# Spreading one row of Q over the partitions: by a store and a 128-fold load in place of a matmul

## The chip, the cores and the metric

The kernel runs on one core of a Trainium2 chip. The core has five instruction streams that the profile names: TensorE (PE, with its weight loads as PEld), VectorE (DVE), ScalarE (ACT), GpSimd (POOL) and SyncE (SP), which here only issues transfers; a "q" behind the name (SPq) is the engine's sequencer. The metric is the device time of one execution in microseconds (us). Lower is better.

## The reference: what is computed

```python
def _attn_ref(x):                       # x: (8, 3008, 256)
    X = np.fft.fft(x, axis=1)
    X = np.fft.fft(X, axis=2)
    return X.real.astype(np.float32)

def _moe_ref(x, w_gate, w_val, w_out):  # x: (24064, 256), d_ff = 1536
    g = x @ w_gate
    silu = g * (1.0 / (1.0 + np.exp(-g)))
    val = x @ w_val
    return (silu * val @ w_out).astype(np.float32)
```

The real part of a two-dimensional Fourier transform over sequence and model dimension goes, as 8 x 3008 = 24064 rows of 256, through a gated feed-forward block. Inputs and output are f32 in device memory.

## The kernel before, in words

The transform over the sequence is done by matmuls with tables of sines and cosines, after the input rows have been folded by their symmetry. The transform over the model dimension is multiplied into the weights once, at the start. Symmetry also halves the rest: for each pair of mirrored output rows the kernel holds one column of `Pt` (cosine part) and one of `Qt` (sine part), both bf16 with 128 partitions; the row is one combination of the two and its mirror row the other. There are 8 x 1504 = 12032 such columns.

They are cut into 24 tiles: tile 0 and tile 3 of 480 columns, tile 23 of 320 (and 8 special columns behind them), the others of 512. For each tile the loop goes over the 12 blocks of 128 hidden features. One (tile, block) is a *unit*, `(t, f)`; there are 288, written out in program order by the loop at lines 930 to 960. Each engine runs its own instructions in that order and waits on semaphores for the others.

A unit has these parts:

- `part_a` (lines 746 to 791): matmuls of the gate `g` and the value `v` (line 756), Silu on ACT, the product `hp` for the row.
- `part_b` (lines 793 to 808), one unit later: the matmuls that turn the accumulated sums into the mirror row's (line 799), Silu again, the product `hm`.
- `OWork` (lines 695 to 726): of the tile before, eight 128x256 output matmuls (line 722) per unit. A pair of 128-row blocks is ready every three units; `evict` (line 679) copies it from PSUM to a buffer `ev` on ACT (line 682; the pool has four buffers, line 649) and SP stores it (line 688).
- At some units, the fold of later input on POOL (lines 160 to 191), loads of `XA` and `XC` for it on SP's queue (lines 128 to 147, dealt out by `run_loads`, line 835), and `transform` (line 566), which makes the next tiles' `Pt` and `Qt`; DVE writes them at line 611. A tile's last `Qt` columns are written at units 5 and 6 of the tile before, at the latest.

From tile 3 on, some units are *split* (lines 733 to 744 and 762 to 784): blocks 0, 2, 4, 6, 8 and 10, and in the last tiles eight of twelve. There the value's even part `e` and odd part `o` are kept apart: DVE forms `es = bc * w0[f] + e` (line 769), then `vp = es - o/2` (line 775) and `vm = es + o/2` (line 778 or 781), and POOL multiplies by the Silu.

`bc` is row 0 of `Qt` (the model dimension's term d = 0) on all 128 partitions. `spread_row0` (line 920) makes it: a matmul with `sel`, whose row 0 is all ones and the rest zero, into a PSUM tile of the pool `o` (line 923), and an ACT copy to SBUF in f32 (line 926). It is called for tile 3 ahead of unit (3, 0), and for each tile t + 1 from 4 to 23 ahead of unit (t, 11), the last of the tile before: 21 times. The first reader is line 769 of the next tile's unit 0. The pool `bc` has two buffers.

SP's queue is in order: it issues the output stores, each after ACT's copy, and the input loads, each after its buffer is free. Transfers on this queue take turns on eight semaphores, and each waits for the eighth before it.

Of the kernel before, what the change touches and what calls it, by code (L numbers as in the profile page):

```python
# [12 lines left out]
F32 = mybir.dt.float32  # L13
I32 = mybir.dt.int32
BF16 = mybir.dt.bfloat16
# [16 lines left out]
def kernel(  # L32
# [8 lines left out]
    nc = tc.nc  # L41
    B, M, D = x.shape
    Dff = moe_w_gate.shape[1]
    P = 128
# [4 lines left out]
    nF = Dff // P  # L49
    T = 512  # L50
# [6 lines left out]
    nT = len(wide)  # L57
# [9 lines left out]
    def width(t):  # L67
        return wide[t]
# [22 lines left out]
    sel = const.tile([P, P], BF16, name="sel")  # L91
# [24 lines left out]
    def rows_at(b, row, ap):  # L116
        return bass.AP(tensor=x.tensor, offset=(b * M + row) * D, ap=ap)
# [4 lines left out]
    def down_set(b, a, j, L, n):  # L122

        return rows_at(b, R * (a + 1) - 2 * j, [[2 * L * D, n], [-2 * D, L], [1, 2 * D]])
# [125 lines left out]
    for hi in range(2):  # L250
        q.dma_start(out=XC3[64 * hi:64 * hi + NCR, 0:2, :],
                    in_=rows_at(0, 2 * (P + 1) - 1 + 2 * hi * R, [[2 * D, NCR], [R * D, 2], [1, 2 * D]]))
    for hi in range(2):
        for a in range(2):
            q.dma_start(out=XC3[64 * hi:64 * hi + NCR, 2 + a, :],
                        in_=down_set(0, 3 - 2 * hi - a, JC, LC, NC_))
    q.dma_start(out=XC0[NCR:64 + NCR + 1:64, 0:2, 1],
                in_=rows_at(0, 0, [[2 * R * D, 2], [R * D, 2], [1, D]]))
# [21 lines left out]
    for i in range(6):  # L280
        ps = psO.tile([P, T], F32, name="o")
# [253 lines left out]
    def pq_tiles(t):  # L535
        if t not in ptile:
            w = width(t) + B if t == nT - 1 else T
            ptile[t] = (pqp if t < nT - 1 else const).tile([P, w], BF16, name="Pt")
            qtile[t] = (pqp if t < nT - 1 else const).tile([P, w], BF16, name="Qt")
        return ptile[t], qtile[t]  # L540
# [101 lines left out]

    hp = ctx.enter_context(tc.tile_pool(name="ht", bufs=2))
    sgp = ctx.enter_context(tc.tile_pool(name="sg", bufs=3))
    sgv = ctx.enter_context(tc.tile_pool(name="sgv", bufs=4))
    esp = ctx.enter_context(tc.tile_pool(name="es", bufs=2))
    bcp = ctx.enter_context(tc.tile_pool(name="bc", bufs=2))
# [42 lines left out]
    def run_evicts():  # L690
        for fn in evicts:
            fn()
        evicts.clear()
# [36 lines left out]
    state = {}  # L730
    owork = None

    SPLIT = {0: "H", 2: "H", 4: "P", 6: "P", 8: "P", 10: "H"}
    SPLIT_END = {0: "P", 1: "P", 3: "P", 4: "P", 6: "P", 7: "P", 9: "P", 10: "P"}
    t_end = tile_of((B - 1) * H) - 1

    bc = {}

    def split(u):

        t, f = u
        if t < 3 or (t == nT - 1 and f > 9):
            return None
        return (SPLIT if t < t_end else SPLIT_END).get(f)

# [47 lines left out]
    def part_b(u):  # L793
        t, f = u
        w = width(t)
        Pt, Qt = pq_tiles(t)
        g, v = state.pop(u)
        for gv, ps in ((0, g), (1, v))[:1 if split(u) else 2]:
            nc.tensor.matmul(ps[:, :w], Wm[:, gv, f * P:(f + 1) * P], Qt[:, :w], start=False, stop=True,  # L799
                             skip_group_check=True)  # L800
        if split(u) == "P":
            sg = sgv.tile([P, T], F32, name="sgv")
            nc.scalar.activation(sg[:, w - 1::-1], g[:, :w], AF.Silu)  # L803
            nc.gpsimd.tensor_tensor(hts[t][1][:, f, :w], sg[:, :w], v[:, :w], op=Alu.mult)  # L804
            return
        sg = sgp.tile([P, T], F32, name="sg")
        nc.scalar.activation(sg[:, :w], g[:, :w], AF.Silu)  # L807
        nc.vector.tensor_tensor(hts[t][1][:, f, w - 1::-1], sg[:, :w], v[:, :w], op=Alu.mult)  # L808
# [26 lines left out]
    def run_loads(i):  # L835

        if not loads:
            credit[0] = 0
            return
        credit[0] += 7 if loads[0][0][0] == "A" else 5 if i >= 2 * nF else 12  # L840
        while loads and credit[0] >= loads[0][2]:
            credit[0] -= loads[0][2]
            loads.pop(0)[3]()
# [7 lines left out]
    def items_a(b):  # L851
        return [(("A", b), 0, 2 if k < NA else 4, fn) for k, fn in enumerate(load_a(b, nc.sync))]
# [6 lines left out]
    def fold_step(what, i, unit):  # L859
        kind, b = what  # L860
        q, j = divmod(i, 6)
        if j == 0:
            load_all(what, q)
            if kind == "A":
                queue[what] = fold_steps(nc.gpsimd, XA, *coef_a(b), q, slice(0, P))
            else:
                bb = 1 if b == 1 else q
                queue[what] = fold_steps(nc.gpsimd, XC, *coef_c(b), bb, slice(0, P), q_down=bb)
        queue[what].pop(0)()
        if q == LASTQ[kind, b == 1] and j == 0:  # L870
            act_at.setdefault(max(unit + 2, 11), []).append(what)

    def load_next(what):
        kind, b = what
        if kind == "A":
            if b + 1 < B:
                at = next((k for k, ((kd, c), *_) in enumerate(loads) if kd == "C" and c > b + 1), len(loads))
                loads[at:at] = items_a(b + 1)
        else:
            b = b // 2 * 2 + 2  # L880
            if b < B:
                loads.extend(items_c(b))
# [36 lines left out]

    def spread_row0(t):  # L920
        ps = psO.tile([P, T], F32, name="o")
        w = width(t) + (B if t == nT - 1 else 0)
        nc.tensor.matmul(ps[:, :w], sel, pq_tiles(t)[1][:, :w], start=True, stop=True)  # L923
        bc.pop(t - 2, None)
        bc[t] = bcp.tile([P, T], F32, name="bc")
        nc.scalar.copy(bc[t][:, :w], ps[:, :w])

    prev = None
    owork = None
    for i, u in enumerate(units):  # L930
        t, f = u
        if (t, f) == (3, 0):
            spread_row0(t)
        if 3 <= t < nT - 1 and f == nF - 1:
            spread_row0(t + 1)
        for fn in before.pop(i, ()):
            fn()
        if i == 10:
            loads[0:0] = items_a(1)
        run_loads(i)  # L940
        odd = part_a(u)
        if owork:
            owork.run(4)
        if odd:
            odd()
        if prev is not None:
            part_b(prev)
            run_evicts()
            if prev[1] == nF - 1:
                owork = OWork(prev[0], hts[prev[0]])  # L950
                owork.run(4)
        if owork and not (prev is not None and prev[1] == nF - 1):
            owork.run(4)
        for what, j in fold_at.get(i, ()):
            fold_step(what, j, i)
        for what in act_at.pop(i, ()):
            load_next(what)
        if i in job_at:
            transform(*job_at[i])
        prev = u  # L960
# [38 lines left out]
```

## Time and profile before

| | |
|---|---|
| median of 3 runs | 665.38 us (665.36 to 665.39) |
| profiled execution | 665.54 us |
| its span, first to last instruction | 663.8 us |
| granted TensorE clock, mean | 0.999 |
| PE busy | 652.4 us (98%) |
| DVE busy | 541.2 us (82%) |
| POOL busy | 482.5 us (73%) |
| ACT busy | 427.7 us (64%) |
| bytes moved by DMA | 52.56 MB, mean 79 GB/s |

The busy time of an engine is the union of its instructions' times. Matmuls overlap their neighbours, so a single matmul's length in the profile is longer than the distance from its start to the next one's. "A <- B" in a list of waits means that an instruction of A stood idle until B had finished; the figures are the sum in us, the times it happened and the longest. In the chain of work that ended last, each step is followed back to what released it. A timeline row has the start in us, the length in us, engine, line, operation, output and inputs, and a count of merged instructions. Rows by window have the window, its length, then the busy time and count of PE, PEld, DVE, ACT and POOL, the granted clock, the DMA engines' busy share and GB/s.

### The profile page before, as it was taken

To read this page: it belongs to the slowest core of one execution; us is meant where nothing else is said; L and a number is where in the kernel's file an instruction comes from. 1 tells how busy PE (TensorE), PEld (TensorE's weight loads), DVE (VectorE), ACT (ScalarE), POOL (GpSimd) and SP (SyncE) were. 2 spreads that over 40 slices of the span, in tenths; PEclk is the share of its full clock that TensorE was granted. 3 is DMA by queue.
4 is the path that set the end of the run, shared out by engine and by line. 5 is a ranking of instruction groups with operands and counts; after the bars stand their busy time and mean duration, and the time that the engine had idled before them with its cause. 6 is when DMAs were issued, how large, how long until landed. Compare 5 with 4: busy or idle time off the path is not lost.

```text
span 663.8 us, 13324 instructions
## 1 busy us (share of the span) xinstructions
PE 652.4 (98%) x4366; PEld 413.0 (62%) x4366; DVE 541.2 (82%) x976; ACT 427.7 (64%) x762; POOL 482.5 (73%) x507
## 2 busy tenths in 40 slices
PE   7999999999999999999999999999999999999997
PEld 5446666666656666666666666656666666666676
DVE  7786668888888888888888888888889888888872
ACT  7576566666666666666666666666666666666663
POOL 9890952988678789785786777885776668877871
PEclk9999999999999999999999999999999999999999
DMA  9554223525312261245225211124111111111112
GB/s 231 105 93 114 75 88 89 159 71 121 109 56 64 78 150 60 64 108 124 60 67 136 76 33 49 35 77 128 49 33 49 33 46 35 49 32 49 48 49 73
DMA packets 49767, 52.56 MB, mean 79 GB/s; under 512 B 7130, under 2 KB 41026, under 8 KB 49698
## 3 DMA queue, kind: packets, MB, share of 16 engines
q1 hardware_dynamic: 46514, 49.35, 27.3%
q0 software_dynamic: 3184, 2.36, 2.4%
q8 instruction: 34, 0.56, 0.4%
q14 instruction: 35, 0.29, 0.2%
HBM read 29.39 MB, written 24.65 MB: 81 GB/s over the span
## 4 chain that ended last, share of the span: by engine, by line
PE 93%; DMA 3%; DVE 2%; SPq 1%; issue 0%; ACT 0%; DVEq 0%; ACTq 0%
PE o L722 37%; PE g L756 18%; PE v L756 18%; PE g L799 9%; PE v L799 5%; PE v L579 3%; DMA XC<-in_x_dram 2%; PE g L579 1%; DMA XA<-in_x_dram 1%; PE o L923 1%; SPq L144 1%; DVE Qt L611 1%; DVE hp L790 0%; DVE hm L808 0%; SPq L141 0%
## 5 line engine op out<-in xcount | busy, mean ns | idle before, releaser
L782 POOL TENSOR_TENSOR hp<-sgv,vv 128x512 bf16<-128x512 f32 (+2 forms) x135 | 169.1, 1252 | 109.2 <-DVE vv L775 94.9
L807 ACT ACTIVATE sg<-g 128x512 f32<-128x512 f32 (+2 forms) x201 | 118.8, 591 | 83.0 <-PE g L799 66.0
L722 PE MATMUL o<-Wo,hp 128*128 128x256 bf16 (+2 forms) x1140 | 169.6, 273 | 0.0
L722 PE MATMUL o<-Wo,hm 128*128 128x256 bf16 (+2 forms) x1140 | 169.6, 273 | 0.0
L808 DVE TENSOR_TENSOR hm<-sg,v 128x512 bf16<-128x512 f32 (+2 forms) x201 | 135.1, 672 | 21.9 <-ACT sg L807 21.9
L722 PEld LDWEIGHTS <-hp 128*128 128x128 bf16 (+2 forms) x1140 | 112.0, 98 | 63.5
L722 PEld LDWEIGHTS <-hm 128*128 128x128 bf16 (+2 forms) x1140 | 112.0, 98 | 63.2 <-issue 0.4
L769 DVE SCALAR_TENSOR_TENSOR es<-bc,w,v 128x512 f32<-128x512 f32 (+2 forms) x135 | 98.7, 731 | 30.3 <-PE v L756 30.1
L804 POOL TENSOR_TENSOR hm<-sgv,vv 128x512 bf16<-128x512 f32 (+2 forms) x87 | 107.0, 1239 | 16.9 <-ACT sgv L803 16.4
L790 DVE TENSOR_TENSOR hp<-sg,v 128x512 bf16<-128x512 f32 (+2 forms) x153 | 102.6, 671 | 13.4 <-ACT sg L789 11.4
L789 ACT ACTIVATE sg<-g 128x512 f32<-128x512 f32 (+2 forms) x153 | 90.3, 590 | 31.4 <-PE g L756 29.7
L756 PE MATMUL g<-Pt,Wp 128*128 128x512 bf16 (+2 forms) x288 | 108.2, 376 | 0.3 <-DVE Qt L611 0.3
L756 PE MATMUL g<-Qt,Wq 128*128 128x512 bf16 (+2 forms) x288 | 107.9, 375 | 0.5 <-DVE Qt L611 0.5
L756 PE MATMUL v<-Pt,Wp 128*128 128x512 bf16 (+2 forms) x288 | 107.9, 375 | 0.0
L799 PE MATMUL g<-Qt,Wm 128*128 128x512 bf16 (+2 forms) x288 | 107.8, 374 | 0.0
L775 DVE SCALAR_TENSOR_TENSOR vv<-v,es 128x512 f32<-128x512 f32 (+2 forms) x135 | 91.8, 680 | 17.9
L766 ACT ACTIVATE sgv<-g 128x512 f32<-128x512 f32 (+2 forms) x135 | 80.0, 593 | 23.2 <-PE g L756 18.2
L756 PEld LDWEIGHTS <-Wp 128*128 128x128 bf16 x576 | 56.3, 98 | 43.9 <-issue 7.4
L803 ACT ACTIVATE sgv<-g 128x512 f32<-128x512 f32 (+2 forms) x87 | 50.8, 584 | 47.3 <-PE g L799 39.4
L799 PE MATMUL v<-Qt,Wm 128*128 128x512 bf16 (+2 forms) x153 | 57.3, 374 | 2.1 <-DVE hp L790 2.1
L756 PEld LDWEIGHTS <-Wq 128*128 128x128 bf16 x441 | 43.2, 98 | 24.1 <-issue 0.9
L778 DVE SCALAR_TENSOR_TENSOR vv<-v,es 128x512 f32<-128x512 f32 (+2 forms) x87 | 57.6, 662 | 0.0
(173 smaller groups left out, 721.5 us busy)
## 6 DMA issues: line engine op xcount, KB each, us to landing
out_dram<-ev SPq DMA_DIRECT2D x96, 128.0 KB
XA<-in_x_dram SPq DMA_DIRECT2D x32, 256.0 KB
XA<-in_x_dram SPq DMA_DIRECT2D x112, 64.0 KB
XC<-in_x_dram SPq DMA_DIRECT2D x210, 16.0 KB
XC<-in_x_dram SPq DMA_DIRECT2D x56, 60.0 KB
out_dram<-ev SPq DMA_DIRECT2D x12, 120.0 KB
out_dram<-ev SPq DMA_DIRECT2D x10, 112.0 KB
XA<-in_x_dram SPq DMA_DIRECT2D x1, 1024.0 KB
```

Source lines behind the costliest of these rows:

```text
L722: nc.tensor.matmul(ps[:n, j, :], hts[minus][:, f, c:c + n], Wo[:, f, :], start=(f == 0), stop=(f == nF - 1))
L756: nc.tensor.matmul(ps[:, :w], Wt[:, gv, fs], src[:, :w], start=start, stop=stop, skip_group_check=True)
L766: nc.scalar.activation(sg[:, :w], g[:, :w], AF.Silu)
L769: stt(es[:, :w], bc[t][:, :w], w0[:, f:f + 1], e[:, :w], op0=Alu.mult, op1=Alu.add)
L775: stt(vp[:, :w], o[:, :w], -0.5, es[:, :w], op0=Alu.mult, op1=Alu.add)
L782: nc.gpsimd.tensor_tensor(hts[t][0][:, f, :w], sg[:, :w], vp[:, :w], op=Alu.mult)
L789: nc.scalar.activation(sg[:, :w], g[:, :w], AF.Silu)
L790: nc.vector.tensor_tensor(hts[t][0][:, f, :w], sg[:, :w], v[:, :w], op=Alu.mult)
L799: nc.tensor.matmul(ps[:, :w], Wm[:, gv, f * P:(f + 1) * P], Qt[:, :w], start=False, stop=True, skip_group_check=True)
L804: nc.gpsimd.tensor_tensor(hts[t][1][:, f, :w], sg[:, :w], v[:, :w], op=Alu.mult)
L807: nc.scalar.activation(sg[:, :w], g[:, :w], AF.Silu)
L808: nc.vector.tensor_tensor(hts[t][1][:, f, w - 1::-1], sg[:, :w], v[:, :w], op=Alu.mult)
```

## The change

From tile 4 on the matmul and the ACT copy go. In their place `store_row0(t + 1)` ahead of unit (t, 7) stores partition 0 of `Qt` (up to 512 bf16, 1 KB) to a buffer in device memory, and `load_row0(t + 1)` ahead of unit (t, 9) loads that row into all 128 partitions of a `bc` tile (128 KB written). Both are issued on SP's queue; the load waits for the store's landing, and behind it in the queue stand the loads of that unit and the output stores of unit 9. `bc` becomes bf16, as `Qt` is. Line 769 of the next tile waits for the load. Tile 3 keeps its matmul, with a bf16 copy. A new pool `rd` of two buffers in device memory is added.

```diff
+    rdp = ctx.enter_context(tc.tile_pool(name="rd", bufs=2, space=bass.MemoryType.DRAM))
...
+    ROW0 = (7, 9)
...
     def spread_row0(t):
         ps = psO.tile([P, T], F32, name="o")
+        w = width(t)
+        nc.tensor.matmul(ps[:, :w], sel, pq_tiles(t)[1][:, :w], start=True, stop=True)
+        bc[t] = bcp.tile([P, T], BF16, name="bc")
+        nc.scalar.copy(bc[t][:, :w], ps[:, :w])
+
+    row0d = {}
+
+    def store_row0(t):
         w = width(t) + (B if t == nT - 1 else 0)
-        nc.tensor.matmul(ps[:, :w], sel, pq_tiles(t)[1][:, :w], start=True, stop=True)
-        bc.pop(t - 2, None)
-        bc[t] = bcp.tile([P, T], F32, name="bc")
-        nc.scalar.copy(bc[t][:, :w], ps[:, :w])
+        row0d[t] = rdp.tile([1, T], BF16, name="row0")
+        nc.sync.dma_start(out=row0d[t][:, :w], in_=pq_tiles(t)[1][0:1, :w])
+
+    def load_row0(t):
+        w = width(t) + (B if t == nT - 1 else 0)
+        bc[t] = bcp.tile([P, T], BF16, name="bc")
+        nc.sync.dma_start(out=bc[t][:, :w], in_=row0d.pop(t)[0, :w].partition_broadcast(P))
...
-        if 3 <= t < nT - 1 and f == nF - 1:
-            spread_row0(t + 1)
+        if 3 <= t < nT - 1 and f in ROW0:
+            (store_row0, load_row0)[ROW0.index(f)](t + 1)
```

## The prediction

> **What bounds the kernel now.** I read the page first (busy shares, granted clock, the chain that ended last), then the waits of TensorE (PE), then PE's own instructions around the removed one.
>
> ```profile
> span 663.8 us, 13324 instructions
> PE 652.4 (98%) x4366; PEld 413.0 (62%) x4366; DVE 541.2 (82%) x976; ACT 427.7 (64%) x762; POOL 482.5 (73%) x507
> ...
> PEclk9999999999999999999999999999999999999999
> ...
> PE 93%; DMA 3%; DVE 2%; SPq 1%; issue 0%; ACT 0%; DVEq 0%; ACTq 0%
> PE o L722 37%; PE g L756 18%; PE v L756 18%; PE g L799 9%; PE v L799 5%; PE v L579 3%; DMA XC<-in_x_dram 2%; PE g L579 1%; DMA XA<-in_x_dram 1%; PE o L923 1%; SPq L144 1%; DVE Qt L611 1%; DVE hp L790 0%; DVE hm L808 0%; SPq L141 0%
> ```
>
> PE is busy 98% of the span at a full granted clock, and 93% of the chain is PE. Line 923, the matmul that the change removes, is itself on that chain. Busy time can flatter a pipelined engine, so the waits decide. These are PE's waits on other engines from 131 to 652 us, which is tile 4 to just before the drain, and in the same stretch DVE's wait at line 769:
>
> ```profile
> PE v L756 <- DVE vv L778: 1.0, 2, 0.6
> ```
> ```profile
> DVE es L769 <- PE v L756: 29.1, 42, 0.8
> ```
>
> In 521 us PE waited 1.0 us for others, in two places, while DVE, the nearest rival for the bound, waited for PE. So in the tiles that change, the time is the spacing of PE's instructions, and a PE instruction less gains its spacing.
>
> **The change, part by part.**
>
> *Twenty matmuls go (tiles 4 to 23; tile 3 keeps its own).* All 21 of today, their weight loads, and the ACT copies behind them:
>
> ```profile
> L923 PEld LDWEIGHTS <-sel x21: 97/98/98, 103.6 to 629.7; 128*128 128x128 bf16 x21
> L923 PE MATMUL o<-Qt,sel x21: 303/379/379, 103.8 to 629.8; 128*128 128x512 bf16 x19, 128*128 128x480 bf16 x1, 128*128 128x328 bf16 x1
> ```
> ```profile
> L926 ACT COPY bc<-o x21: 432/587/592, 104.2 to 630.2; 128x512 f32<-128x512 f32 x19, 128x480 f32<-128x480 f32 x1, 128x328 f32<-128x328 f32 x1
> ```
>
> The 379 ns is not the price: it is one matmul's length from start to end, and the next starts before it ends. The price is the distance of the starts, from the timeline of PE at the end of tile 5 and of tile 22:
>
> ```profile
> 179.83 0.60 PE L722 MATMUL o<-Wo,hm 128*128 128x256 bf16 x4
> 180.26 0.38 PE L923 MATMUL o<-Qt,sel 128*128 128x512 bf16 x1
> 180.48 0.38 PE L756 MATMUL g<-Pt,Wp 128*128 128x512 bf16 x1
> 180.70 0.38 PE L756 MATMUL g<-Qt,Wq 128*128 128x512 bf16 x1
> 180.91 0.38 PE L756 MATMUL v<-Pt,Wp 128*128 128x512 bf16 x1
> ...
> 629.83 0.30 PE L923 MATMUL o<-Qt,sel 128*128 128x328 bf16 x1
> 629.97 0.38 PE L756 MATMUL g<-Pt,Wp 128*128 128x512 bf16 x1
> ```
>
> From 180.26 to 180.91 are three steps, 0.217 us each. Tiles 4 to 22 are 512 wide: 19 x 0.217 = 4.12 us. Tile 23 has 328 columns: 629.97 - 629.83 = 0.14. Sum 4.26 us, all on the path. The weight loads (98 ns) lie under the matmul before and add nothing; if each stood open, the gain would be 20 x 0.098 = 2.0 us more.
>
> The Trainium skill gives another price: "TensorE: Matmul & The Clock Gate", section "Back-to-back issue gap", has about 131 ns per matmul of 512 columns sustained in a stream with weight loads, and 216 ns for the isolated one. By the first the sum would be an estimated 20 x 0.131 = 2.6 us. The trace has a stream with weight loads at 217 ns, so the trace decides.
>
> *Twenty ACT copies go:* 20 x 0.587 = 11.7 us of ACT, which is 64% busy and not on the chain; worth 0. As cover for PE it only gains. POOL waited for these copies 2.9 us:
>
> ```profile
> POOL hp L782 <- DVE vv L775: 94.9, 71, 3.2
> ...
> POOL hp L782 <- ACT bc L926: 2.9, 3, 1.1
> ```
>
> but POOL waits 94.9 us for DVE in the same list (131 to 663 us), so this too frees nothing. The list holds no wait for a transfer.
>
> *DVE reads bf16 in place of f32* (line 769), and its first such instruction of a tile waits for the load's semaphore:
>
> ```profile
> L769 DVE SCALAR_TENSOR_TENSOR es<-bc,w,v x135: 548/741/749, 104.9 to 647.2; 128x512 f32<-128x512 f32 x122, 128x328 f32<-128x328 f32 x7, 128x480 f32<-128x480 f32 x6
> L769 DVEq EVENT_SEMAPHORE  x1: 50/50/50, 104.8 to 104.8; - x1
> ```
>
> The instruction's other input stays f32 in PSUM; I take its 741 ns unchanged. The extra wait instruction is at most 20 x 0.05 = 1.0 us of DVE, on an engine that has 29.1 us of waits for PE here: 0, with 1.0 us as the upper end.
>
> *Forty transfers join SP's queue.* SP's other work, and where it stands idle:
>
> ```profile
> L688 SPq DMA_DIRECT2D out_dram<-ev x279: 254/359/1224, 59.1 to 660.9; - x140
> ```
> ```profile
> SPq L688 <- ACT ev L682: 299.2, 81, 7.5
> ...
> SPq L141 <- DMA XC<-in_x_dram: 5.8, 11, 0.9
> ```
>
> Issuing costs 40 x 0.36 = 14 us of SP. SP waits 299.2 us for the copies of line 682, up to 7.5 at once, and hides it. The load also waits in SP's queue until its store has landed. Behind it stand the output stores of unit 9 and, in tiles with input traffic, loads of XA and XC. The output stores may be late without harm: evO has four buffers, one taken every three units, so only a delay of many microseconds reaches ACT and then PE. For late input loads the folds on POOL would wait; POOL waits for no transfer in its list above. Cost 0. The store itself waits for DVE's last write of Q, which is done before SP arrives, as the next rows show.
>
> *Does the row arrive in time?* No row shows this pair of transfers, so I bound each landing. SP reaches the store after the output stores of unit 6, and the row is needed at the next tile's first es. Tile 19 to 20 (little traffic), 3 to 4 and 12 to 13 (the heaviest):
>
> ```profile
> 545.25 1.14 SPq L688 DMA_DIRECT2D out_dram<-ev  x3
> ```
> ```profile
> 123.03 1.01 SPq L688 DMA_DIRECT2D out_dram<-ev  x2
> ...
> 359.26 1.61 SPq L688 DMA_DIRECT2D out_dram<-ev  x3
> ```
> ```profile
> 543.04 1.33 DVE L611 TENSOR_TENSOR Qt<-g,od 128x160 bf16<-128x160 f32 x7 [1.21 <-PE g L756]
> ...
> 556.45 0.75 DVE L769 SCALAR_TENSOR_TENSOR es<-bc,w,v 128x512 f32<-128x512 f32 x1 [0.80 <-PE v L756]
> ```
> ```profile
> 131.37 0.74 DVE L769 SCALAR_TENSOR_TENSOR es<-bc,w,v 128x512 f32<-128x512 f32 x1
> ...
> 370.02 0.74 DVE L769 SCALAR_TENSOR_TENSOR es<-bc,w,v 128x512 f32<-128x512 f32 x1
> ```
>
> Q is written by 544.4, SP is free at 546.4, es starts at 556.45: 10.1 us, less two issues of 0.36, leaves 9.3 us for two landings. In tile 12 to 13 it is 370.02 - 360.87 = 9.1 us, in tile 3 to 4 131.37 - 124.04 = 7.3 us. What a landing takes, from the chain (a small load alone; the megabyte and a small load behind it, at the start of the run), and the traffic in the three places:
>
> ```profile
> 1.98 5.97 DMA XA<-in_x_dram
> ...
> 26.50 1.95 DMA XC<-in_x_dram
> ```
> ```profile
> 0.00:25.00 25.00, 21.50 (x145) 13.18 (x146) 16.83 (x59) 16.65 (x24) 22.25 (x49) 1.00 0.91 205
> ...
> 119.00:127.00 8.00, 8.00 (x57) 5.33 (x55) 6.99 (x13) 5.37 (x11) 8.00 (x9) 1.00 0.77 217
> 361.00:368.00 7.00, 7.00 (x46) 4.37 (x45) 5.93 (x10) 4.69 (x9) 6.08 (x8) 1.00 0.75 199
> 545.00:556.50 11.50, 10.89 (x72) 6.86 (x71) 9.72 (x17) 7.37 (x14) 8.20 (x7) 1.00 0.15 46
> ```
>
> (The last two columns are the DMA engines' busy share and GB/s; the first line is the start of the run.) Lower end 1.95 us each, upper end 5.97 us each. In a quiet tile the share is 0.15, so 1.95 is the near row: 2 x 1.95 + 0.7 = 4.6 us of 10.1, some 5 us to spare. In tile 3 to 4 four XA loads (1.05 MB) and two output stores (0.26 MB) go ahead of the row: 1.31 MB at 217 GB/s is 6.0 us from 119.35, plus 1.95, so the store lands near 127.3; the load, 0.4 + 1.95 + 0.6 (128 KB at that rate), near 130.3, about 1 us before es. Tile 12 to 13 has 2 us or more to spare. So 0 in every tile; with the upper end for one of the two landings in the two heavy tiles, 1 to 2 us late in all.
>
> *Sum:* -4.26 us. The profiled execution took 665.54 us (span 663.8 and 1.7 around it), 0.16 above the median of the runs; 665.54 - 4.26 = 661.28, and against the median 661.1.
>
> **Rivals.**
>
> 1. *The row is late in the heavy tiles.* For it: DMA shares of 0.77 and 0.75, and only 7.3 us in tile 3 to 4. Against it: the sums above. It costs some 1.2 us: 662.3. The Trainium skill speaks for it ("DMA: Bandwidth & Descriptors", section "Queues, rings and completion order"): descriptors of one queue are consumed in ring order on each DMA engine, so a small row would queue behind the XA loads; the trace's bytes ahead of it were priced so above.
>
> 2. *The row is late in every tile: slower.* DVE's queue is in order, so a late es holds DVE, then POOL's hp and the v buffers PE needs. It decides where the two landings take over 9.3 us together in quiet tiles, and eats the gain at 9.5 (20 x 0.21 us). At 10 us each tile loses 0.7: 665.4 - 4.3 + 14 = 675. For it: at the upper end, 2 x 5.97 = 11.9, it happens. Against it: that price is from a share of 0.91 at the start of the run, here 0.15.
>
> 3. *No gain:* the tile's pace is DVE's or POOL's, and PE only gets idle time: 665.4. For it: DVE is 82% busy and caused both of PE's waits. Against it: 1.0 us of waits in 521.
>
> 4. *A weight load comes into the open.* Before, the weights of the next tile's first matmul load under line 923 (0.217 us); after, under the last matmul of line 722, whose starts are 0.43 / 4 = 0.109 us apart. If its 98 ns then stand open, a tile gains 0.217 - 0.098 = 0.119 and the whole 2.4 us: 663.0. Against it: 0.098 fits under 0.109, and lines 722 follow each other at that distance all through. The skill's 131 ns, named above, would come to nearly the same time.
>
> 5. *The whole 379 ns is won:* 20 x 0.379 = 7.6 us, 657.8. For it: nothing but the duration row.
>
> **How the numbers follow.** Forecast 0.75; rival 1, 0.08; rival 2, 0.08; rival 3, 0.05; rival 4, 0.03; rival 5, 0.01. Faster by over 0.2% (1.3 us, about what a measurement of this kernel can tell from no change) are the forecast and rivals 1, 4 and 5: 0.87. Same: 0.05. Slower: 0.08. The forecast's own range is 661.1 with 1.0 us down (PE's two waits vanish) and 1.0 us up (the upper end of the wait instructions); I take 660.1 to 663.0, which adds rivals 1 and 4 and leaves out 2, 3 and 5, 0.14.
>
> **What would show it.** Right: line 923 left once, PE's spacing from the last line 722 of a tile to the first line 756 without a gap, PE's waits near 1.0 us, no wait of es on the bc load, SP's wait for line 682 shrunk by roughly the load's wait for its store (20 x 2 us). Wrong: a row "DVE es <- DMA bc", or PE waiting for vv or hp at the first units of a tile, or POOL's L168 waiting for XA or XC.

## The result, and the profile after

The changed kernel takes 661.88 us (median of 4 runs, 661.67 to 662.33) against 665.38 us before: ratio 0.9949, 95% interval 0.9936 to 0.9961, so 3.5 us faster by the medians (2.6 to 4.3 by the interval). In the later series on one chip it is 662.06 against 665.97, ratio 0.9942 (0.9930 to 0.9955), 3.9 us. The forecast was 661.1, a gain of 4.26 us. The direction and the mechanism held; 0.8 us of the gain is missing in the first series and 0.35 us in the second, and the experiments are mostly about that part.

Lines behind the new pool have moved by one to thirteen: 722 is now 723, 756 is 758, 769 is 771, 799 is 801, 803 is 805; the store is line 934 and the load line 939. The page of the changed kernel, answering to the lines shown of before:

```profile
span 659.8 us, 13360 instructions
PE 649.1 (98%) x4346; PEld 411.5 (62%) x4346; DVE 539.4 (82%) x976; ACT 418.1 (63%) x742; POOL 481.7 (73%) x507
...
PE 93%; DMA 3%; DVE 2%; SPq 1%; issue 0%; ACT 0%; DVEq 0%; ACTq 0%
PE o L723 37%; PE g L758 18%; PE v L758 18%; PE g L801 9%; PE v L801 5%; PE v L579 3%; DMA XC<-in_x_dram 2%; PE g L579 1%; DMA XA<-in_x_dram 1%; SPq L144 1%; DVE Qt L611 1%; DVE hp L792 0%; SPq L141 0%; DVE hm L810 0%; PE o L452 0%
```

PE has 20 matmuls fewer, is as busy as before, and the removed line has left the chain; no other line has taken its share. PE's waits on other engines from 131 to 648 us, and DVE's in that stretch:

```profile
PE v L758 <- DVE vv L780: 1.0, 2, 0.6
```
```profile
DVE es L771 <- PE v L758: 28.1, 42, 0.8
...
DVE vv L777 <- POOL BBc L189: 0.5, 1, 0.5
```

PE still waits 1.0 us, in the same two places, and there is no row of es waiting for the load. SP's waits now (the page of its queue):

```profile
SPq L689 <- ACT ev L683: 263.3, 77, 7.5
SPq L939 <- DMA row<-Qt: 10.8, 9, 2.0
```

The wait for ACT's copies is 36 us shorter than before (299.2). Issuing the forty transfers takes 12.3 us of that, and the loads' waits for their stores 10.8 us; the rest lies in other rows of the list. SP had the time.

The seam between tile 5 and tile 6 in PE's timeline:

```profile
179.28 0.60 PE L723 MATMUL o<-Wo,hm 128*128 128x256 bf16 x4
179.72 0.38 PE L758 MATMUL g<-Pt,Wp 128*128 128x512 bf16 x1
179.93 0.38 PE L758 MATMUL g<-Qt,Wq 128*128 128x512 bf16 x1
```

Line 758 starts 0.44 us after the four matmuls of line 723, where line 923 started before. The hole is closed without a gap. I matched PE's 4346 common matmuls one by one in the two traces and noted each place where the distance to the trace of before changes by more than 0.03 us. Behind the noise of the first 16 us there are these:

```
step (us)   times   where
-0.216      19      first matmul of tiles 4 to 22 (-0.215 to -0.216)
-0.139       1      first matmul of tile 23
+0.14        2      transform's gate matmul, line 579, at 223 and 383 us of before
+0.06, +0.07 2      v <- Qt,Wm (line 758), in tiles 8 and 10
start: -0.10        line 402, behind the first XC transfer (15.15 before, 15.05 after)
sum: -3.93
```

### The profile page after: what moved, and what is told of

Read it like the earlier page. It is cut to its first block, busy times and chain, and to the rows that moved or that the text cites. A ratio compares the mean times of both kernels' runs of the same rounds, so it can differ in the third digit from the quotient of the medians.

```text
span 659.8 us, 13360 instructions
## 1 busy us (share of the span) xinstructions
PE 649.1 (98%) x4346; PEld 411.5 (62%) x4346; DVE 539.4 (82%) x976; ACT 418.1 (63%) x742; POOL 481.7 (73%) x507
## 4 chain that ended last, share of the span: by engine, by line
PE 93%; DMA 3%; DVE 2%; SPq 1%; issue 0%; ACT 0%; DVEq 0%; ACTq 0%
PE o L723 37%; PE g L758 18%; PE v L758 18%; PE g L801 9%; PE v L801 5%; PE v L579 3%; DMA XC<-in_x_dram 2%; PE g L579 1%; DMA XA<-in_x_dram 1%; SPq L144 1%; DVE Qt L611 1%; DVE hp L792 0%; SPq L141 0%; DVE hm L810 0%; PE o L452 0%
## 5 line engine op out<-in xcount | busy, mean ns | idle before, releaser
L810 DVE TENSOR_TENSOR hm<-sg,v 128x512 bf16<-128x512 f32 (+2 forms) x201 | 135.1, 672 | 20.9 <-ACT sg L809 20.9
L771 DVE SCALAR_TENSOR_TENSOR es<-bc,w,v 128x512 f32<-128x512 bf16 (+2 forms) x135 | 98.8, 732 | 29.3 <-PE v L758 29.1
L758 PE MATMUL v<-Qt,Wq 128*128 128x512 bf16 (+2 forms) x153 | 57.4, 375 | 0.0
```

The source lines that it names most:

```text
L758: nc.tensor.matmul(ps[:, :w], Wt[:, gv, fs], src[:, :w], start=start, stop=stop, skip_group_check=True)
L771: stt(es[:, :w], bc[t][:, :w], w0[:, f:f + 1], e[:, :w], op0=Alu.mult, op1=Alu.add)
```

## The experiments

**The changed kernel again, and four ways to take it apart.** The later series named above, five rounds on one chip, has this run and the next ones, up to the kernel with both matmuls and transfers, all against the same runs of the kernel before (665.97 us). The first of it is the changed kernel itself.

> The changed kernel once more, to see how far its single times lie apart (661.67 to 662.33 so far, against 665.36 to 665.48 before the change). Theory A, the gain is the 20 removed matmul spacings less two waits of the transform's gate matmul for a PSUM buffer that the planner chose otherwise (0.14 us each): 661.4 in most executions, and a later one needs another cause. Theory B, the transfers cost time by their traffic and their place in SP's queue: 661.7 to 662.3, spread over 0.5 us. Theory C, the row is late for line 771 in some executions: the same spread, with a wait of es for the bc load in a profile that is slow.

Measured: 662.06 us (661.92 to 662.40), 3.9 us under before. The kernel before spread here from 665.28 to 666.21, as widely as any variant, so theories B and C lose the argument they had from the spread. C loses its other sign too: this profile has no wait of es for the load, and the row lands at least 1.01 us before es in every tile. A's absolute figure missed: the whole series, the kernel before included, runs 0.6 us later than the first one. By the gain, A expected 4.0 us and 3.9 were measured. Part of the scatter can be seen: in the profiles of this series line 402, near the beginning, starts anywhere from 15.18 to 15.51 us.

**Neither matmul nor transfers.** From tile 4 on this kernel leaves out each tile's own row 0: line 769 reads the row of tile 3.

```diff
+    bcfix = bcp.tile([P, T], BF16, name="bcfix")
...
-        bc[t] = bcp.tile([P, T], BF16, name="bc")
-        nc.scalar.copy(bc[t][:, :w], ps[:, :w])
+        for k in range(t, nT):
+            bc[k] = bcfix
+        nc.scalar.copy(bcfix[:, :w], ps[:, :w])
+        nc.scalar.copy(bcfix[:, w:], zero.to_broadcast([P, T - w]))
...
-        if 3 <= t < nT - 1 and f in ROW0:
-            (store_row0, load_row0)[ROW0.index(f)](t + 1)
```

> Neither matmul nor transfers from tile 4 on: line 769 reads tile 3's row in every tile, so the d=0 term is left wrong. This measures the removed matmuls alone; the planner's PSUM buffers are those of before. All theories: 665.4 - 4.26 = 661.1, single times within 0.15 us. If it is 661.7 or more, the matmuls were worth less than their spacing.

Measured: 661.49 us (661.35 to 661.78), 4.48 under before, ratio 0.9934 (0.9921 to 0.9948). The profiled span is 659.6 against 663.8, 4.2 us. The removed matmuls are worth their spacing, as all theories had it by the gain; the absolute 661.1 is missed with the whole series, and the single times lie 0.43 us apart where I expected 0.15.

**Transfers, but nobody reads the row.** As the last, with the calls of store and load kept and the load going into a tile of its own:

```diff
-        bc[t] = bcp.tile([P, T], BF16, name="bc")
-        nc.sync.dma_start(out=bc[t][:, :w], in_=row0d.pop(t)[0, :w].partition_broadcast(P))
+        bcu[t] = bcp.tile([P, T], BF16, name="bc")
+        nc.sync.dma_start(out=bcu[t][:, :w], in_=row0d.pop(t)[0, :w].partition_broadcast(P))
```

> Stores and loads as in the change, but nothing reads the loaded row (line 769 reads tile 3's), and the planner's PSUM buffers are those of before. Theory A: 661.1, as with neither. Theory B, traffic and SP's queue cost: 661.6 to 662.0, with the spread of the changed kernel. Theory C, late rows: 661.1 and no spread, since nobody waits for the row.

Measured: 661.52 us (661.15 to 661.93), 4.45 under before, ratio 0.9935 (0.9922 to 0.9947). The absolute figure is near theory B's 661.6, but the kernel with neither stands at 661.49 in the same series: beside it, the transfers cost 0.03 us. Matched matmul by matmul, the two traces differ by one step over 0.03 us: 0.10 at line 402, before the first store. Theory B falls.

**Matmuls and transfers.** The kernel before, with the store and the load added beside its matmul and copy:

```diff
+        if 3 <= t < nT - 1 and f in ROW0:
+            (store_row0, load_row0)[ROW0.index(f)](t + 1)
...
+        bcu[t] = bup.tile([P, T], BF16, name="bu")
+        nc.sync.dma_start(out=bcu[t][:, :w], in_=row0d.pop(t)[0, :w].partition_broadcast(P))
```

> The kernel before with its matmuls and copies kept (bc in bf16), and the same stores and loads added beside them into a tile that nothing reads. Theories A and C: 665.4, as before. Theory B: 665.9 to 666.3.

Measured: 665.79 us (665.63 to 666.24), ratio 1.0000 (0.9991 to 1.0008). The same answer from the other side: matched with the trace of before, it ends 0.22 us later, and 0.22 us is the step at line 402. Its profile has PE's wait unchanged at 1.0 us (131 to 652 us):

```profile
PE v L761 <- DVE vv L783: 1.0, 2, 0.6
```

So what the changed kernel (662.06) loses against the unread row (661.52) goes with the reading, as far as it is not scatter. The matched traces of these two differ by 0.61 us: 0.14 at each of the two gate matmuls, 0.07 and 0.05 in tiles 8 and 10, and 0.21 at line 402, near the beginning, which varies from run to run. That leaves 0.40 us for the reading. At the first gate matmul, PE in the trace of before and in the changed kernel's, and ACT in the latter:

```profile
223.06 0.33 PE L579 MATMUL v<-Tab,CEa 128*128 128x189 bf16 x2
223.23 0.33 PE L560 MATMUL v<-Tab,CEa 128*128 128x189 bf16 x2
223.39 0.33 PE L579 MATMUL g<-Tab,CEa 128*128 128x189 bf16 x2
```
```profile
222.08 0.33 PE L579 MATMUL v<-Tab,CEa 128*128 128x189 bf16 x2
222.25 0.33 PE L560 MATMUL v<-Tab,CEa 128*128 128x189 bf16 x2
222.55 0.33 PE L579 MATMUL g<-Tab,CEa 128*128 128x189 bf16 x2
```
```profile
221.90 0.60 ACT L805 ACTIVATE sgv<-g 128x512 f32<-128x512 f32 x1 [0.55 <-PE g L801]
```

Before, the gate matmul follows line 560 after 0.16 us. After, it comes 0.30 us behind and starts at 222.55, just when the Silu of line 805 ends (221.90 + 0.60 = 222.50). The built programs tell why: the pool of gate accumulators has three PSUM buffers, and here two are about to come free, one that DVE frees and one that this Silu frees. Before, the planner gave the transform the first, and it does so in the kernels where nothing reads the loaded row; where line 771 depends on the load it gives it the second, here and once more at 383 us. Of the main loop's buffers none other moved but those of the gate (from the first of these points to the second) and of the output accumulators, which lost the removed tile.

**The buffers put back.** The transforms of unit (7, 5) and (13, 5) take over the gate tile of the transform one unit earlier:

```diff
-        ps = given or {eo: [pool.tile([P, T], F32, name=nm) for pool, nm in ((psV, "v"), (psG, "g"))] for eo in eos}
+        ps = given or {eo: [psV.tile([P, T], F32, name="v"), gkeep.pop((b, part), None) or psG.tile([P, T], F32, name="g")]
+                        for eo in eos}
+        if (b, part) in ((3, 0), (5, 0)) and eos == (0,) and not given:
+            gkeep[b, part] = ps[0][1]
```

> The change, with the PSUM buffers of the gate put back to those of before: the transform at unit (7, 5) and the one at (13, 5) take over the gate buffer of the transform one unit earlier, which DVE frees, in place of the one that ACT's mirror Silu frees. Theory A: the two waits of 0.14 us go, the starts of PE stand as with the unread row, and the time is 0.3 to 0.4 us under the changed kernel's, some 661.5 to 661.7 where the kernel before takes 665.97. If the difference between the changed kernel and the unread row (0.5 us) comes from waiting for the row: no better than the changed kernel, 662.0.

Measured: 661.67 us (661.60 to 661.91) against 665.80, ratio 0.9937 (0.9923 to 0.9951). In PE's timeline the gate matmul is back at its distance (line 579 is 584 here):

```profile
222.59 0.33 PE L584 MATMUL v<-Tab,CEa 128*128 128x189 bf16 x2
222.75 0.33 PE L560 MATMUL v<-Tab,CEa 128*128 128x189 bf16 x2
222.92 0.33 PE L584 MATMUL g<-Tab,CEa 128*128 128x189 bf16 x2
```

Matched against the unread row, both steps of 0.14 us are gone and the small ones in tiles 8 and 10 remain (0.06 and 0.08). The trace settles it. The time agrees in direction (4.13 us under before, where the changed kernel was 3.91 under), but the intervals overlap, so the 0.2 us cannot be told by times alone. Its median is the lowest of the kernels here that compute the whole reference.

**The row brought later.** The same change with other units, one round each.

```diff
-    ROW0 = (7, 9)
+    ROW0 = (9, 11)
```

> The load two units later (store ahead of unit 9, load ahead of unit 11), so it stands behind the output stores of unit 9. In the changed kernel's trace these end some 3.2 us before es in quiet tiles, and a load takes 2.9 us: margin about 0 to 0.3 us, and none where XA and XC loads stand between. If the row's lateness is what decides: 662 to 666, with waits of es for the bc load in busy tiles. If the row has more time than its landing shows: 662.0.

Measured: 682.24 us (681.51 to 682.96), ratio 1.0246 (1.0226 to 1.0265): slower than before, and far outside what I expected. DVE's waits in its profile:

```profile
DVE es L771 <- PE v L758: 28.1, 43, 1.3
DVE es L771 <- DMA bc<-row: 20.3, 12, 3.6
```

By the landing of each load (the last update of its semaphore in the trace) es starts 0.10 us behind it in 19 of the 20 tiles: these now wait for their row. In tile 15 es starts 0.28 us behind the landing and no later than in the changed kernel. My margin of 0 to 0.3 us took the load's landing as 2.9 us everywhere; it was 2.9 to 4.1 here, and between the output stores of unit 9 and the load stand the input loads of unit 10 in busy tiles.

How much of the lateness PE pays can be read tile by tile. I took as lateness how much later than in the changed kernel es starts behind the matmul `v <- Pt,Wp` before it (0.34 to 0.57 us there), and as loss how much longer it takes from that matmul to the next tile's. Es is late by 24.4 us in all, up to 3.6 in a tile, and the loss is 19.5 us: in most tiles the lateness less 0.3 us. (The wait row's 20.3 us counts 12 of the tiles only; that it comes so near to 682.24 - 661.88 = 20.4 us of time is chance.)

```diff
-        if 3 <= t < nT - 1 and f in ROW0:
-            (store_row0, load_row0)[ROW0.index(f)](t + 1)
+        if 3 <= t < nT - 1 and f == 11:
+            store_row0(t + 1)
+            load_row0(t + 1)
```

> Store and load both ahead of unit 11, behind the output stores of unit 9. The landing of the store (1.3 us) now comes on top: the row lands about 1.2 us after es could start in quiet tiles, 2 us in busy ones. If a late es holds PE by its full lateness: 662 + 20 x 1.2 = 686, slower than before. If the v buffers give PE slack for part of it: between 670 and 680. It tells where rival 2 begins and what a late row costs per microsecond.

Measured: 716.95 us (716.15 to 717.74), ratio 1.0767 (1.0746 to 1.0787). DVE's wait for the load and PE's for es:

```profile
DVE es L771 <- DMA bc<-row: 47.8, 17, 5.1
```
```profile
PE v L758 <- DVE es L771: 33.0, 19, 4.1
PE v L758 <- DVE hm L810: 4.1, 11, 0.4
PE v L758 <- DVE vv L780: 3.7, 7, 0.6
```

55 us over the changed kernel, 2.75 us per tile, where I had 1.2 to 2. By the same reckoning es is late by 53.0 us in all (1.0 to 5.2 in a tile) and the loss is 54.1 us. The v buffers give PE little slack, some 0.3 us in a tile: then PE stands at the next line 758 for es itself, and what is later than that passes through one to one. Five tiles lose more than their lateness; the last section comes back to them.

## Why the prediction was right

*What bounds the kernel:* right. PE's starts set the time, and with 1.0 us of waits on other engines in 521 us every PE instruction taken out in tiles 4 to 23 came off the time. Rival 3, no gain, is out.

*The price of the matmuls:* right to 0.02 us. The steps are 19 x 0.216 and 0.139, together 4.24 us, where the prediction had 4.26 from three distances of starts. The kernel with neither confirms it by time (4.48, with an interval of 3.5 to 5.3) and by span (4.2). The length of 379 ns (rival 5) would have given 7.6. The isolated gap of 216 ns in the Trainium skill, "TensorE: Matmul & The Clock Gate", section "Back-to-back issue gap", is what this stream shows, weight loads and all; its sustained 131 ns per matmul is not, and neither is rival 4, since no weight load came into the open.

*ACT's copies, the bf16 read:* worth 0, as said. Line 771 has the mean of 732 ns that line 769 had with 731.

*Forty transfers in SP's queue:* cost 0, as said, shown twice: 0.03 us without the matmuls and -0.18 us (ratio 1.0000) with them, and no step in the matched traces behind line 402. SP's wait for the copies shrank by 36 us, near the 40 us foretold (20 x 2 us), but that is partly luck: the loads stood only 10.8 us for their stores, in nine of the tiles from 14 on, since in the others input loads fill the time between store and load.

*Whether the row arrives in time:* right, and rival 1 did not happen. The landings in the changed kernel's trace, from the updates of the semaphores:

```
tile   store lands after   load issued   load lands   es starts   margin (us)
 4     2.45                126.09        129.18       131.04      1.85
 8     1.37                230.11        234.25       236.82      2.57
13     1.37                361.97        366.00       368.02      2.01
20     1.90                545.25        548.10       553.08      4.99
22     1.28                596.49        599.37       604.55      5.18
```

Tile 4 and tile 13 have the least, as the bounds had it (about 1 us and 2 us or more); quiet tiles have 3.4 to 5.4 where the prediction had some 5. Tile 4 has little to spare: 1.01 us in the second profile of this kernel and 0.49 us in that with the buffers put back. Stores landed in 1.1 to 2.5 us, with the lower bound of 1.95 between; loads took 2.8 to 4.1, well above it, and nowhere the upper bound of 5.97.

*Rival 2* did not happen, but as a mechanism it is real: two units later it makes the kernel slower than before. The prediction put DVE, POOL's hp and the v buffers between a late es and PE. In the last two experiments PE stands for es itself, and all of the lateness but some 0.3 us in a tile reaches the time.

*What was missed:* the prediction costed the extra wait of line 771 at nothing, with 1.0 us as the upper end. As an instruction on DVE it is small. But the dependence on a transfer also changed which PSUM buffer the planner gives two transforms, and PE waits 2 x 0.14 = 0.28 us more there. This was not a term of the sum at all. A further 0.13 us, in tiles 8 and 10, goes with the reading of the row and not with the gate buffers. DVE and PE in tile 8 of the changed kernel:

```profile
238.04 0.69 DVE L777 SCALAR_TENSOR_TENSOR vv<-v,es 128x512 f32<-128x512 f32 x1 [0.48 <-POOL BBc L189]
...
240.44 0.68 DVE L810 TENSOR_TENSOR hm<-sg,v 128x512 bf16<-128x512 f32 x1
```
```profile
241.18 0.38 PE L758 MATMUL v<-Qt,Wm 128*128 128x512 bf16 x1
```

The late matmul starts 0.06 us behind the end of hm, and 0.05 us in tile 10; with the unread row it does so too, but there hm ends earlier, since vv did not stand still. The stands of vv in tiles 8 and 10, 0.48 to 0.50 us each, are in all three traces in which the row is read and comes in time, and in none of the four without this reading. What vv stands for is open: the profile names POOL's line 189 in tile 8 and PE's line 801 in tile 10, and with the unread row vv started before the same row of line 189 had begun.

With the two, 4.24 - 0.28 - 0.13 = 3.83 us against 3.9 in the second series. Why the first series has 3.5 was not separated; line 402 alone starts up to 0.5 us apart between profiles. The range, 660.1 to 663.0, held the result for another reason than the prediction gave: its 1.0 us upwards stood for wait instructions on DVE. That is luck.

## What to carry to other kernels

Price a matmul in a saturated stream by the distance of the starts around it, not by its length; matching two traces instruction by instruction then shows to some hundredths of a microsecond what was won and where it was given back. A transfer in place of compute is free only up to the instruction that needs it: note the margin per tile, the busiest tile first, and count what stands ahead of it in the issuing queue, since behind that point a late microsecond costs nearly a microsecond in each tile. A new dependence can also move buffers in a pool that the diff does not touch, so compare the buffers of the two built programs too.

## What the runs showed that I had not expected

The kernel before is itself not steady over series: 665.36 to 665.48 in the first, 665.28 to 666.21 in the second. Much of that may be the first XC transfer, behind which line 402 started from 15.05 to 15.55 us in the profiles here.

A 1 KB store to device memory landed sooner (1.1 to 1.5 us in most tiles) than the 1.95 us of the smallest load in the chain of before, while a 128 KB load of one row to 128 partitions took at least 2.8 us. The Trainium skill, "DMA: Bandwidth & Descriptors", section "Anatomy of one DMA", has about 2.0 us fixed plus bytes over 436 GB/s, measured on the GpSimd path, not on SP's queue; by that an estimated 2.0 and 2.3 us. In the changed kernel's trace 18 of the 20 stores lie below the one and all loads above the other.

With PE standing at each tile's start, the granted clock fell in the kernel with both transfers ahead of unit 11:

```profile
core 0: 714.4 us, clock 0.985
```

The changed kernel had 1.000. Tile by tile, the clock was 0.90 to 0.95 in tiles 4, 5, 6, 10 and 16 and 1.00 in the fifteen others. In the trace it is 0.5 for 3.41 us in each of the first four and for 6.83 us in tile 16, which begin during or up to 1.3 us after a stand of PE of 2.0 to 4.1 us; tile 8, with a stand of 3.6 us, kept the full clock. The fifteen tiles lose 28.4 us for 32.1 us of lateness, the five 25.7 us for 20.9. At the fifteen's rate of 0.25 us less than the lateness in a tile, the five would lose 19.6 us; the difference, an estimated 6 us of the 55, goes with the clock.
